# Chunked attention and token routing on one core: all comparisons on VectorE, one selection a batch, a new order of steps

## The chip, the cores and the metric

The kernel runs on one core of a Trainium2 chip. A core has TensorE (PE, matrix products), VectorE (DVE), ScalarE (ACT), GpSimd (POOL) and SyncE (SP); each works through its own queue of instructions in order, and waits on semaphores for the others. Transfers run on 16 DMA engines. The metric is the device time of one execution in microseconds; lower is better.

## The reference

Inputs are q, k, v of shape 4 x 8 x 768 x 64 (batch, head, position, width), 8 memory keys and values for each head, and for the second part a gate vector of 512, w1 (512 x 1024), w2 (1024 x 512) and the capacity 128.

```python
for c in range(24):                              # chunks of 32 queries
    l, r = max(0, 32*c - 16), min(768, 32*c + 40)
    K = concat(mem_k, k[:, :, l:r]); V = concat(mem_v, v[:, :, l:r])
    s = q[:, :, 32*c:32*c+32] @ K.T / 8
    a = exp(s - max(s)); a = a / (sum(a) + 1e-9)
    out[:, :, 32*c:32*c+32] = a @ V
x = out.transpose(0, 2, 1, 3).reshape(4, 768, 512)
for b in range(4):
    score = x[b] @ w_gate                        # 768 scores
    top = indices of the 128 largest scores
    h = relu(x[b, top] @ w1)
    x[b, top] += sigmoid(score[top])[:, None] * (h @ w2)
```

The output is x, 4 x 768 x 512 in float32.

## The kernel before

**Units of work.** The 32 heads are taken two at a time, as 16 pairs n = 0 to 15; four pairs make a batch b. Everything that is done is a step with a short name, and a long string, ORDER, lists all 600 steps as `name.number.engine` (a ACT, v DVE, g POOL, p PE, s SP). The program runs through the list once and issues the instructions of each step, so the list sets the order on every engine's queue. No scheduler moves anything afterwards.

**Loads.** LK, LQ, LV (lines 130 to 150) load keys, queries and values with GpSimd DMAs that turn float32 into float16; pairs 0 and 1 come singly, later ones two at a time (LK.2 brings pairs 2 and 3, and is called K2 below). There are five buffers of each. MK and MV add the memory rows, on SP's queue from pair 2 on. LW.0 to LW.3 (line 170) load the weights w1 and w2.

**Attention for a pair.** TQ, TK, TV (`tr`, line 285) turn q, k, v on TensorE into PSUM; QB or EQ, EK and EV evict them (`copy`, lines 119 to 125). S multiplies queries by keys, R takes the largest score of each row on VectorE, A subtracts it on TensorE, E is the exponential on ScalarE. PT turns the result, EP0 and EP1 evict it. W0 and W1 turn the value windows, with the products with the gate vector, and E0, E1, VG evict those. PV is the product with the values (SG its gate columns alone, for the last batch), RC the reciprocal of the sums, GP the part of the routing score that this pair gives, NM the normalized output. ST.b writes the batch's 768 rows to DRAM, with six DMAs on SP's queue.

**Routing for a batch b.** mSC sums the 768 scores into `scr`, 128 x 6. mB0, mB1 spread them along rows on TensorE, and mR0, mR1 evict those into `brow`, so that each partition holds all 768 scores in float32. mC0 to mC5 (`cmp_`, line 545) compare the 768 scores with six columns of `scr`, one instruction each, and write 128 x 768 values of 0 or 1; mT0 to mT5 (line 555) count them with TensorE, so that each token knows how many tokens beat it. mMK makes the mask of those with fewer than 128 above them. mIN, mLT and mSL (line 576) number the chosen ones. mSE (line 583) makes the selection matrix by comparing a row of the numbers 1 to 128 with each token's slot, in six instructions of 128 x 128. mAU reads the indices and the gate out of it, mIX and mGS evict them. mGX and mGD compute the gate 1/(1+exp(-score)): the exponential on ScalarE, then an addition, a reciprocal (on VectorE always) and two small operations (lines 534 to 537).

**The block for a batch.** For b = 0 to 2 mGI gathers the 128 chosen rows back from DRAM (GpSimd, indirect) and mGT turns them; for the last batch mG0 to mG3 gather them by products with the selection matrix from a float16 copy (XC). mX evicts, mFa and mFb (line 643) are the products with w1, mHa and mHb the relu, mYa and mYb (lines 673, 678) the products with w2, mY scales by the gate, and mSCAT (line 690) adds the rows to the output in DRAM, as an indirect DMA from GpSimd. The scatters follow one another, since they write the same tensor.

**What stood where.** Of the 24 comparisons 12 were on VectorE and 12 on GpSimd: all six of batch 0, three of batch 1, one of batch 2 and two of batch 3. The selections of batches 0 and 1 were on GpSimd, those of 2 and 3 on VectorE.

Of the kernel before, what the change touches and what calls it, by code (L numbers as in the profile page):

```python
# [8 lines left out]
FP = mybir.dt.float32  # L9
F16 = mybir.dt.float16  # L10
# [33 lines left out]
NM.8.v mR1.1.a mB0.1.p E.10.a TV.11.p EK.11.v PV.9.p mR0.1.a EK.12.v mFa.0.p EV.11.a mC2.1.v mC1.1.g
mFb.0.p RC.9.v GP.9.v mC3.1.v mHa.0.a mC0.1.g PT.10.p NM.9.v TV.12.p EP0.10.a mYa.0.p mHb.0.v S.11.p
EP1.10.v mT0.1.p mT1.1.p R.11.v mT2.1.p W0.11.p mC5.1.g mYb.0.p mC4.1.v EV.12.a PV.10.p mY.0.v mT3.1.p
mT4.1.p mT5.1.p W0.12.p RC.10.v mSCAT.0.g W1.11.p mMK.1.v E0.11.a GP.10.v TK.13.p E0.12.v E1.11.a W1.12.p
VG.11.v EK.13.v TQ.13.p E1.12.a A.11.p mIN.1.v EQ.13.v TQ.12.p TV.13.p E.11.a VG.12.v EQ.12.v mLT.1.p
TV.14.p NM.10.v EV.13.a S.12.p PT.11.p mSL.1.v R.12.v mSE.1.g S.13.p EP0.11.a TQ.14.p EV.14.v A.12.p
EP1.11.a W0.13.p E.12.a EQ.14.v TK.14.p mAU.1.p E0.13.v PT.12.p R.13.v TK.15.p PV.11.p EP0.12.a mIX.1.v  # L50
mGS.1.v mGI.1.g A.13.p RC.11.v EK.14.a GP.11.v mSC.2.v NM.11.v E.13.a mB0.2.p ST.2.s mB1.2.p mR0.2.a
mR1.2.v EP1.12.a S.14.p mC0.2.v mC2.2.g mC3.2.v mGX.2.a W1.13.p EK.15.a mC1.2.v SG.12.p mGD.2.g R.14.v
VG.13.a TQ.15.p mGT.1.p EQ.15.a E1.13.v A.14.p W0.14.p mX0.1.v W1.14.p mFb.1.p RC.12.v E0.14.v E.14.a
VG.14.v TV.15.p GP.12.v E1.14.v mT0.2.p mT1.2.p mHb.1.a mT2.2.p mT3.2.p mFa.1.p mC4.2.v EV.15.a mC5.2.v
mT4.2.p PT.13.p mT5.2.p mHa.1.a S.15.p mMK.2.v PV.12.p EP0.13.a mIN.2.v R.15.v mLT.2.p W0.15.p EP1.13.a
PT.14.p mSL.2.v A.15.p mSE.2.v EP0.14.a mYa.1.p E0.15.v E.15.a mAU.2.p EP1.14.v W1.15.p mIX.2.v PT.15.p
mGI.2.g mGS.2.v VG.15.a NM.12.v SG.13.p EP0.15.a mYb.1.p RC.13.v EP1.15.a E1.15.v SG.14.p GP.13.v mY.1.a
XC.12.g SG.15.p RC.14.v GP.14.v mSCAT.1.g RC.15.v PV.14.p GP.15.v mSC.3.v mGX.3.a mB0.3.p NM.14.v mB1.3.p
mR0.3.a mGD.3.g PV.13.p mR1.3.v mGT.2.p mC0.3.v mC1.3.g PV.15.p mC3.3.v mX0.2.a mT0.3.p NM.13.v mFa.2.p
mC2.3.g mC4.3.v mT1.3.p mFb.2.p mHa.2.a mC5.3.v XC.14.g XC.13.a NM.15.v mT2.3.p mT3.3.p mT4.3.p mT5.3.p  # L60
mYa.2.p mHb.2.a mMK.3.v mIN.3.v ST.3.s XC.15.a mLT.3.p mYb.2.p mSL.3.v mSE.3.v mY.2.a mG0.3.p mG1.3.p
mSCAT.2.g mX0.3.a mG2.3.p mX1.3.a mG3.3.p mX2.3.v mAU.3.p mX3.3.v mGS.3.v mFa.3.p mFb.3.p mHa.3.a mIX.3.v
# [8 lines left out]
def _sap(t, offset, dims):  # L71
    return bass.AP(tensor=t.tensor, offset=t.offset + offset, ap=[list(t.ap[0])] + [list(d) for d in dims])
# [3 lines left out]
def kernel(  # L76
# [280 lines left out]
    QBS = set(range(8))  # L357
# [215 lines left out]
    def mSL(b, e):  # L573
        m = mods[b]
        m.slot = mod2.tile([128, NB], FP, tag="slot", name="slot")
        nc.vector.scalar_tensor_tensor(out=m.slot, in0=m.incl, scalar=m.pn[:, 0:1], in1=m.mask,  # L576
                                       op0=ALU.add, op1=ALU.mult)

    def mSE(b, e):
        m = mods[b]  # L580
        m.sel = mod2.tile([128, NB, cap], F16, tag="sel", name="sel")
        for bl in range(NB):
            (nc.vector if e == DVE else nc.gpsimd).tensor_scalar(out=m.sel[:, bl, :], in0=iota1, scalar1=m.slot[:, bl:bl + 1],  # L583
                                                                 scalar2=None, op0=ALU.is_equal)
# [163 lines left out]
```

## Time and profile before

| | |
|---|---|
| runs shown | 154.9, 156.58, 155.77 us; median 155.77 |
| the profiled execution | 154.68 us, of which the span is 153.0 us |
| granted TensorE clock, mean | 0.877 |
| busy in the span: PE, DVE, ACT, POOL | 115.6, 98.1, 87.9, 76.5 us |
| instructions on DVE, ACT, POOL | 221, 114, 97 |
| software DMA queue: packets, MB | 12320, 13.66 |

A page of a profile shows one execution. Busy times of an engine are shares of the span in which it worked; instructions may overlap by a little at their ends, so the mean duration of one times their number is somewhat more than the busy time. Lines of groups read: source line, engine, operation, output and input tile, shapes, count, then busy time and mean nanoseconds of one, then the idle time of the engine before them and what ended it. Rows of a timeline begin with the start and the duration in microseconds, and end with the idle time before, where there was some, and its releaser. In the slices each digit is a fortieth of the span, in tenths; PEclk is the clock that TensorE was granted.

### The profile page before, as it was taken

The numbers are of one execution on the slowest core, as the hardware profiler recorded it, in microseconds if no ns is written. First come the engines' busy times: TensorE is split into PE (matmuls) and PEld (weight loads), VectorE is DVE, ScalarE is ACT, GpSimd is POOL, SyncE is SP. The second block draws the span as 40 slices with busy tenths as digits, with TensorE's granted clock in tenths as the row PEclk, the third lists the DMA queues.
The fourth block names the chain that finished last, engine by engine and source line by source line (L and its number), as shares of the span: only waits on it lengthen the run. The fifth ranks groups of instructions, "written<-read, shape, count | busy, mean of one in ns | idle before, by whom it ended". The sixth has DMA issues, their size and how long they took to land.

```text
span 153.0 us, 6101 instructions
## 1 busy us (share of the span) xinstructions
PE 115.6 (76%) x2730; PEld 95.2 (62%) x2730; DVE 98.1 (64%) x221; ACT 87.9 (57%) x114; POOL 76.5 (50%) x97
## 2 busy tenths in 40 slices
PE   0367574988689559799699998998849999489800
PEld 0256463977568458688588894976639967377500
DVE  2676562679877978061758899697874684875000
ACT  3962634386945439457499786296944774163400
POOL 6999611333211999940641178628450044983040
PEclk9999959599978955557999999999995999879995
DMA  2998999999999999999834900230570002518631
GB/s 13 163 122 155 195 230 212 205 209 208 209 207 227 287 284 216 217 188 205 139 67 143 350 9 0 20 57 4 202 280 8 4 6 66 69 43 329 112 41 27
DMA packets 16854, 21.91 MB, mean 143 GB/s; under 512 B 1774, under 2 KB 12014, under 8 KB 16829
## 3 DMA queue, kind: packets, MB, share of 16 engines
q0 software_dynamic: 12320, 13.66, 55.6%
q1 hardware_dynamic: 4509, 7.87, 15.3%
q8 instruction: 21, 0.34, 0.9%
q14 instruction: 4, 0.03, 0.1%
HBM read 26.02 MB, written 7.41 MB: 218 GB/s over the span
## 4 chain that ended last, share of the span: by engine, by line
PE 30%; POOL 26%; DMA 14%; issue 8%; ACT 8%; DVE 7%; POOLq 1%; ACTq 0%
POOL cmp L545 14%; DMA ql<-in_q_dram 8%; DMA out_dram<-y,idx 6%; PE p_w L319 3%; PE p_q L285 3%; PE p_v L319 3%; PE p_k L285 3%; PE p_v L285 3%; DVE m L398 2%; PE p_s L403 2%; PE p_x L449 2%; POOL sel L583 2%; PE p_c L555 2%; ACT vT L121 2%; PE p_y L678 2%
## 5 line engine op out<-in xcount | busy, mean ns | idle before, releaser
L545 POOL TENSOR_SCALAR cmp<-brow,scr 128x768 f16<-128x768 f32 x12 | 28.2, 2358 | 11.9 <-ACT brow L121 9.3
L121 ACT COPY pt<-p_p 64x768 f16<-64x768 f16 x19 | 15.1, 793 | 9.0 <-PE p_p L418 7.8
L410 ACT ACTIVATE P<-p_s 128x768 f16<-128x768 f32 x16 | 13.0, 811 | 10.0 <-PE p_s L403 9.8
L285 PE MATMUL p_k<-seg,kl 126*64 126x126 f16 x256 | 12.4, 256 | 6.7 <-DMA kl<-in_mem_k_dram 6.7
L121 ACT COPY vT<-p_v 128x1536 f16<-128x1536 f16 x11 | 15.6, 1440 | 2.8 <-PE p_v L285 2.8
L398 DVE TENSOR_REDUCE m<-p_s 128x12 bf16<-128x768 f32 x16 | 15.2, 951 | 1.8 <-PE p_s L386 0.8
L319 PEld LDWEIGHTS <-vT 128*128 128x128 f16 x192 | 13.6, 107 | 3.2 <-issue 1.2
L478 DVE TENSOR_TENSOR x<-p_x,rd 128x768 f32<-128x768 f32 x16 | 15.1, 946 | 0.2
L285 PEld LDWEIGHTS <-kl 126*64 126x64 f16 x256 | 10.1, 134 | 8.0 <-DMA kl<-in_k_dram 5.7
L449 PE MATMUL p_x<-vw,pt 128*64 128x66 f16 (+2 forms) x480 | 12.2, 199 | 3.7 <-DVE pt L123 2.7
L449 PEld LDWEIGHTS <-pt 128*64 128x64 f16 x480 | 10.5, 119 | 6.1 <-ACT vw L121 2.3
L285 PE MATMUL p_v<-seg,vl 126*64 126x126 f16 x256 | 12.9, 259 | 0.0
L121 ACT COPY kT<-p_k 128x1008 f16<-128x1008 f16 x10 | 10.0, 999 | 5.0 <-PE p_k L285 4.7
L123 DVE COPY qb<-p_q 64x768 f16<-64x768 f16 x14 | 7.7, 552 | 7.1 <-PE p_q L285 4.5
L583 POOL TENSOR_SCALAR sel<-iota,slot 128x128 f16<-128x128 f16 x12 | 7.0, 598 | 10.4 <-DVE slot L576 10.4
L285 PE MATMUL p_q<-ident,ql 96*64 96x96 f16 x256 | 10.0, 231 | 2.8 <-DMA ql<-in_q_dram 2.8
L403 PE MATMUL p_s<-m,negi 128*128 128x384 bf16 x32 | 9.0, 368 | 3.6 <-DVE m L398 3.6
L121 ACT COPY vw<-p_v 128x768 f16<-128x768 f16 x9 | 7.2, 803 | 7.9 <-PE p_v L329 7.0
L545 DVE TENSOR_SCALAR cmp<-brow,scr 128x768 f16<-128x768 f32 x12 | 10.3, 886 | 2.2 <-PE p_c L555 2.0
L418 PE MATMUL p_p<-perm,P 128*128 128x128 f16 x96 | 9.1, 236 | 3.3 <-DVE qb L123 3.2
L690 POOL DMA_INDIRECT out_dram<-y,idx x4 | 6.5, 1628 | 9.4 <-ACT y L684 6.9
L285 PEld LDWEIGHTS <-vl 126*64 126x64 f16 x256 | 10.2, 136 | 1.0 <-issue 0.8
(120 smaller groups left out, 251.1 us busy)
## 6 DMA issues: line engine op xcount, KB each, us to landing
out_dram<-x SPq DMA_DIRECT2D x24, 256.0 KB, 3.4
kl<-in_k_dram POOLq DMA_DIRECT2D x7, 384.0 KB, 16.1
ql<-in_q_dram POOLq DMA_DIRECT2D x7, 384.0 KB, 16.0
vl<-in_v_dram POOLq DMA_DIRECT2D x7, 384.0 KB, 17.3
w_sb<-in_moe_w_dram POOLq DMA_DIRECT2D x4, 512.0 KB, 17.7
kl<-mk SPq DMA_DIRECT2D x7, 120.0 KB, 8.4
vl<-mv SPq DMA_DIRECT2D x7, 100.0 KB
kl<-in_k_dram POOLq DMA_DIRECT2D x2, 192.0 KB, 3.8
```

The costliest lines, as they stand in the source:

```text
L121: nc.scalar.copy(out=out, in_=in_)
L123: nc.vector.tensor_copy(out=out, in_=in_)
L285: nc.tensor.transpose(out=p[64 * h:64 * h + 64, o:o + w], in_=src[n // 2 % GB][0:rows, n % 2, h, 64 * j:64 * j + 64], identity=perm)
L319: nc.tensor.transpose(out=p.bitcast(F16)[:, 128 * o:128 * o + 128], in_=pair(n, 6 * i + o), identity=ident16)
L398: nc.vector.tensor_reduce(out=s.m, in_=keys(s.s), axis=AX.X, op=ALU.max)
L403: nc.tensor.matmul(out=s.s[:, h, 0:384], lhsT=negi, rhs=s.m[:, h, :].unsqueeze(2).to_broadcast([128, NB, 64]), start=False, stop=True, ski ...
L410: nc.scalar.activation(out=s.P, in_=keys(s.s), func=AF.Exp, scale=0.125)
L418: nc.tensor.transpose(out=p[:, 128 * i:128 * i + 128], in_=s.P[:, h, 2 * bp:2 * bp + 2, :].rearrange("p b k -> p (b k)"), identity=perm16)
L449: nc.tensor.matmul(out=X[64 * cc:64 * cc + 64, c2, w * (2 * bp + h):w * (2 * bp + h) + w], lhsT=s.PT[:, i, c, :, :].rearrange("p b t -> p ...
L478: nc.vector.tensor_tensor(out=x5.rearrange("p b g (h d) -> p b g h d", d=D), in0=s.x[:, :, :, :, 0:64], in1=s.rd.unsqueeze(4).to_broadcast ...
L545: (nc.vector if e == DVE else nc.gpsimd).tensor_scalar(out=t, in0=m.brow, scalar1=m.scr[:, bl:bl + 1], scalar2=None, op0=ALU.is_lt)
L583: (nc.vector if e == DVE else nc.gpsimd).tensor_scalar(out=m.sel[:, bl, :], in0=iota1, scalar1=m.slot[:, bl:bl + 1], scalar2=None, op0=ALU ...
```

## The change

Three things change. All 24 comparisons mC0 to mC5 go to VectorE (by the letter in the list). The selection mSE is one instruction for all six columns, with the slots in float16 and broadcast along the row. And the list is a new one, from a search that works with latest times, with the same 600 steps: steps stand in another order on all engines, and some evictions have moved between VectorE and ScalarE. From VectorE to ScalarE go, net, four EP, four EQ, six QB and six VG; from ScalarE to VectorE go four EV, three EK and one of E0, E1; a few set-up steps (CP, CV, CW) move as well, both XC copies of ScalarE go to GpSimd, and batch 0's gate arithmetic mGD goes from VectorE to GpSimd. A function VX and a set VXS come in that are not used, since the set is empty.

```diff
     def mSL(b, e):
         m = mods[b]
-        m.slot = mod2.tile([128, NB], FP, tag="slot", name="slot")
+        m.slot = mod2.tile([128, NB], F16, tag="slot", name="slot")
...
     def mSE(b, e):
         m = mods[b]
         m.sel = mod2.tile([128, NB, cap], F16, tag="sel", name="sel")
-        for bl in range(NB):
-            (nc.vector if e == DVE else nc.gpsimd).tensor_scalar(out=m.sel[:, bl, :], in0=iota1, scalar1=m.slot[:, bl:bl + 1],
-                                                                 scalar2=None, op0=ALU.is_equal)
+        nc.vector.tensor_tensor(out=m.sel, in0=m.slot.unsqueeze(2).to_broadcast([128, NB, cap]),
+                                in1=iota1.unsqueeze(1).to_broadcast([128, NB, cap]), op=ALU.is_equal)
```

Of the list, three places. The loads, only the steps of GpSimd's loads shown (the old list first):

```diff
- LK.0 LQ.0 LV.0 LK.1 LQ.1 LV.1 LK.2 LQ.2 LV.2 LK.4 LQ.4 LV.4 LK.6 LQ.6 LV.6 LW.0 LK.8 LW.1 LQ.8 LW.2 LV.8 LW.3 LK.10 ...
+ LK.0 LQ.0 LV.0 LK.1 LQ.1 LV.1 LW.0 LK.2 LW.1 LQ.2 LW.2 LV.2 LW.3 LK.4 LQ.4 LV.4 LK.6 LQ.6 LV.6 LK.8 LQ.8 LV.8 LK.10 ...
```

The routing of batch 0, its own steps with their engines:

```diff
- mSC.0.v mB1.0.p mB0.0.p mR1.0.v mGX.0.a mR0.0.a mC1.0.g mGD.0.v mC2.0.g mC5.0.g mC0.0.g mT0.0.p mT1.0.p mC3.0.g mT2.0.p mC4.0.g mT3.0.p mT4.0.p mT5.0.p mMK.0.v mIN.0.v mLT.0.p mSL.0.v mSE.0.g mAU.0.p
+ mSC.0.v mB0.0.p mB1.0.p mR0.0.v mR1.0.a mC1.0.v mC0.0.v mGX.0.a mGD.0.g mC3.0.v mC4.0.v mT0.0.p mT1.0.p mC2.0.v mC5.0.v mT2.0.p mT3.0.p mT4.0.p mT5.0.p mMK.0.v mIN.0.v mLT.0.p mSL.0.v mSE.0.v mAU.0.p
```

The end, whole, from mSC.3 on:

```diff
- mSC.3.v mGX.3.a mB0.3.p NM.14.v mB1.3.p mR0.3.a mGD.3.g PV.13.p mR1.3.v mGT.2.p mC0.3.v mC1.3.g PV.15.p mC3.3.v mX0.2.a mT0.3.p NM.13.v mFa.2.p mC2.3.g mC4.3.v mT1.3.p mFb.2.p mHa.2.a mC5.3.v XC.14.g XC.13.a NM.15.v mT2.3.p mT3.3.p mT4.3.p mT5.3.p mYa.2.p mHb.2.a mMK.3.v mIN.3.v ST.3.s XC.15.a mLT.3.p mYb.2.p mSL.3.v mSE.3.v mY.2.a mG0.3.p mG1.3.p mSCAT.2.g mX0.3.a mG2.3.p mX1.3.a mG3.3.p mX2.3.v mAU.3.p mX3.3.v mGS.3.v mFa.3.p mFb.3.p mHa.3.a mIX.3.v mYa.3.p mHb.3.a mYb.3.p mY.3.a mSCAT.3.g
+ mSC.3.v NM.14.v mGX.3.a mB0.3.p mGD.3.g mB1.3.p mR0.3.a PV.15.p mR1.3.v mC0.3.v mY.1.a XC.14.g mC1.3.v mGT.2.p mSCAT.1.g mC2.3.v mT0.3.p mT1.3.p mX0.2.a mC3.3.v mT2.3.p mFa.2.p mC4.3.v mC5.3.v mT3.3.p mT4.3.p NM.15.v mT5.3.p mHa.2.a mFb.2.p mMK.3.v XC.15.g ST.3.s mIN.3.v mLT.3.p mYa.2.p mHb.2.a mSL.3.v mSE.3.v mYb.2.p mG0.3.p mY.2.a mG1.3.p mG2.3.p mX1.3.v mG3.3.p mSCAT.2.g mX0.3.v mX2.3.a mAU.3.p mX3.3.a mFa.3.p mIX.3.v mGS.3.v mFb.3.p mHa.3.v mYa.3.p mHb.3.a mYb.3.p mY.3.a mSCAT.3.g
```

In the old list mSCAT.1.g stands ahead of mSC.3 and of batch 3's gate.

More of the change, by code (lines that the diff above doesn't have):

```diff
@@ L45 @@
[L45 to L59, printed above, removed]
@@ L60 @@
[L60 to L62 removed]
+CV.0.v LK.0.g MK.0.g LQ.0.g C0.0.g LV.0.g CP.4.v CV.4.a CP.3.g CV.2.v CQ.0.a TQ.0.p MV.0.g CP.0.a LK.1.g
+CQ.1.a TK.0.p C1.0.v PM.0.g CV.1.a MK.1.g EK.0.v CP.1.a TV.0.p LQ.1.g QB0.0.v CP.2.a C2.0.g CO.0.v QB1.0.v
@@ new lines @@
+mSC.1.v TV.11.p ST.1.s R.8.v EQ.10.a mB0.1.p EP1.9.a EV.11.v A.8.p S.10.p mR0.1.a W0.10.p R.10.v E.8.a
+mGT.0.p mB1.1.p W0.11.p E0.10.v mX0.0.a A.10.p E0.11.v mR1.1.a TK.11.p mFa.0.p mC0.1.v EK.11.a mC1.1.v
+mFb.0.p mC2.1.v mHa.0.a E.10.a mC4.1.v PT.8.p PV.9.p mHb.0.a EP0.8.v S.11.p mGX.1.a RC.9.v EP1.8.a mGD.1.g
+TK.12.p NM.9.v TK.13.p EK.12.a PT.10.p GP.9.v mYa.0.p EK.13.v R.11.v mYb.0.p EP0.10.a PV.8.p EP1.10.a
+mY.0.v TQ.12.p RC.8.v mSCAT.0.g TK.14.p NM.8.v EQ.12.a A.11.p W1.10.p EK.14.v E.11.a TV.12.p W1.11.p
@@ new lines @@
+W1.14.p mSE.2.v EP0.15.a PV.13.p E1.14.v EP1.15.a mAU.2.p mYa.1.p mIX.2.v NM.13.v VG.14.a mGI.2.g SG.15.p
+SG.14.p RC.15.v GP.15.v mGS.2.v PV.14.p XC.13.g RC.14.v GP.14.v mYb.1.p mSC.3.v NM.14.v mGX.3.a mB0.3.p
+mGD.3.g mB1.3.p mR0.3.a PV.15.p mR1.3.v mC0.3.v mY.1.a XC.14.g mC1.3.v mGT.2.p mSCAT.1.g mC2.3.v mT0.3.p
+mT1.3.p mX0.2.a mC3.3.v mT2.3.p mFa.2.p mC4.3.v mC5.3.v mT3.3.p mT4.3.p NM.15.v mT5.3.p mHa.2.a mFb.2.p
+mMK.3.v XC.15.g ST.3.s mIN.3.v mLT.3.p mYa.2.p mHb.2.a mSL.3.v mSE.3.v mYb.2.p mG0.3.p mY.2.a mG1.3.p
@@ L63 @@
+mG2.3.p mX1.3.v mG3.3.p mSCAT.2.g mX0.3.v mX2.3.a mAU.3.p mX3.3.a mFa.3.p mIX.3.v mGS.3.v mFb.3.p mHa.3.v
 mYa.3.p mHb.3.a mYb.3.p mY.3.a mSCAT.3.g
@@ L355, in QB @@
                  _sap(s.pq[g], 0, [[4, NC], [96, 8], [1, 4]]))
-    QBS = set(range(8))
+    QBS, VXS = set(range(8)), set(())
     def S_(n, e):
```

67 lines of the change are left out of this document (40 added, 27 removed).

## The prediction, on record before the run

> **What bounds the kernel now.** I read the page's slices first, then the busy times by stage, then the chain of waits and the timelines of the two stages that stood out.
>
> ```profile
> span 153.0 us, 6101 instructions
> PE   0367574988689559799699998998849999489800
> PEclk9999959599978955557999999999995999879995
> DMA  2998999999999999999834900230570002518631
> ```
>
> The DMA engines are full for the first nineteen of forty slices (to about 73 us): that is the time of the loads. TensorE is busy nearly all the time after that, but with holes, and its clock is at half around slices 15 to 18. No engine is full, so I cut the span where batch 0's scores are summed (mSC.0, 44.05), where its rows are selected (mSE.0, 74.04) and where the last batch's scores are summed (mSC.3, 127.37).
>
> ```profile
> core 0: us, PE busy (x) PEld busy (x) DVE busy (x) ACT busy (x) POOL busy (x), PEclk, DMA share, GB/s
> 25.80:44.05 18.25, 14.97 (x386) 12.59 (x388) 14.91 (x29) 10.39 (x13) 6.36 (x9) 0.90 1.21 207
> 44.05:74.04 29.99, 25.33 (x542) 21.84 (x541) 18.63 (x36) 17.47 (x22) 17.81 (x13) 0.66 1.20 229
> 74.04:127.37 53.33, 48.17 (x1364) 39.58 (x1364) 41.57 (x99) 38.94 (x51) 23.88 (x27) 0.97 0.32 92
> 127.37:153.00 25.63, 14.53 (x219) 10.77 (x211) 9.22 (x23) 7.11 (x13) 11.42 (x9) 0.87 0.41 93
> 55.00:72.00 17.00, 15.92 (x308) 13.78 (x308) 8.22 (x17) 11.76 (x14) 11.80 (x9) 0.53 1.21 218
> 108.00:115.00 7.00, 4.84 (x140) 4.18 (x141) 5.81 (x11) 4.71 (x8) 3.56 (x4) 1.00 0.72 265
> 115.00:120.00 5.00, 5.00 (x98) 4.64 (x95) 2.11 (x6) 2.61 (x4) 0.00 (x0) 0.66 0.02 5
> ```
>
> The second stage is the poor one: 30 us in which VectorE and ScalarE work 18 us each and TensorE looks full only because its clock is 0.66. The chain of waits and the timeline say why.
>
> ```profile
> 51.88 2.22 POOL cmp L545
> 54.75 4.40 POOL cmp L545 x2
> 59.80 4.40 POOL cmp L545 x2
> 64.25 0.32 PE p_c L555 x6
> ```
>
> ```profile
> 51.61 2.53 DVE L536 CAST aux<-gt 128x6 f16<-128x6 f32 x1
> 55.15 0.80 PE L418 MATMUL p_p<-perm,P 128*128 128x128 f16 x6 [3.21 <-DVE qb L123]
> ```
>
> Six comparisons on GpSimd, one behind the other, carry the chain to 64.2. One of them also holds a VectorE copy of six values per partition for 2.53 us; the query eviction behind it is late, TensorE stands 3.21 us, and after that it runs at 0.53 from 55 to 72. The same happens in small near 112: a comparison holds back batch 2's gate on GpSimd, VectorE waits for the gate, and TensorE idles and then has a slow 115 to 120.
>
> ```profile
> 109.50 2.94 POOL L545 TENSOR_SCALAR cmp<-brow,scr 128x768 f16<-128x768 f32 x1 [2.08 <-DVE brow L123]
> 112.42 0.23 POOL L534 TENSOR_SCALAR gt<-gt 128x6 f32<-128x6 f32 x1
> 112.69 0.19 DVE L535 RECIPROCAL gt<-gt 128x6 f32<-128x6 f32 x1 [0.93 <-POOL gt L534]
> ```
>
> **The change part by part.** The prices, by element count and engine:
>
> ```profile
> L545 DVE TENSOR_SCALAR cmp<-brow,scr x12: 604/784/1261, 89.1 to 134.3; 128x768 f16<-128x768 f32 x12
> ```
>
> ```profile
> L545 POOL TENSOR_SCALAR cmp<-brow,scr 128x768 f16<-128x768 f32 x12 | 28.2, 2358 | 11.9 <-ACT brow L121 9.3 <-DVE brow L123 2.1 <-PE p_c L555 0.5
> L478 DVE TENSOR_TENSOR x<-p_x,rd 128x768 f32<-128x768 f32 x16 | 15.1, 946 | 0.2
> L123 DVE COPY pt<-p_p 64x768 f16<-64x768 f16 x13 | 7.2, 555 | 4.5 <-ACT pt L121 2.5 <-PE p_p L418 1.7
> L583 POOL TENSOR_SCALAR sel<-iota,slot 128x128 f16<-128x128 f16 x12 | 7.0, 598 | 10.4 <-DVE slot L576 10.4
> L123 DVE COPY vT<-p_v 128x1536 f16<-128x1536 f16 x5 | 5.3, 1051 | 0.9 <-PE p_v L285 0.8
> L123 DVE COPY kT<-p_k 128x1008 f16<-128x1008 f16 x6 | 4.0, 674 | 0.4 <-PE p_k L285 0.4
> L468 DVE RECIPROCAL rd<-p_x 128x12 f32<-128x12 f32 x16 | 3.6, 227 | 4.0 <-PE p_x L449 3.9
> L123 DVE CAST vw<-p_v 128x24 f16<-128x24 f32 x11 | 2.9, 260 | 1.9 <-ACT vw L121 1.6 <-PE p_v L329 0.3
> L472 DVE TENSOR_TENSOR scp<-p_x,rd 128x12 f32<-128x12 f32 x16 | 2.7, 167 | 0.3
> ```
>
> Comparisons: GpSimd loses 12 (28.2 us) and VectorE gains 12. Its own took 0.604 to 1.261 us, the median 0.784. I take 0.784, since the slow ones ran beside GpSimd's, which are gone: +9.4 us on VectorE, bounds +7.2 and +15.1. Selection: six instructions a batch become one over 768 values. No row shows that form; it lies between the fastest comparison (0.604) and the 768-wide product (0.946), and I take 0.946, the only row with two tensor inputs. GpSimd loses its 7.0 us. These are loads on engines; the path is decided by the order, which I price by stage.
>
> *Stage A, start to mSC.0.* The new order issues all four weight loads ahead of LK.4; the old one began them after LV.6. GpSimd's issues are paced by landings, eight transfers deep, which shows what each load costs:
>
> ```profile
> 26.05 0.73 POOL L172 DMA_DIRECT2D w_sb<-in_moe_w_dram  x1 [4.44 <-DMA ql<-in_q_dram]
> 29.60 0.71 POOL L172 DMA_DIRECT2D w_sb<-in_moe_w_dram  x1 [1.20 <-DMA kl<-in_k_dram]
> 37.75 0.75 POOL L176 DMA_DIRECT2D w_sb<-in_moe_w_dram  x1 [1.67 <-DMA ql<-in_q_dram]
> 42.37 0.67 POOL L138 DMA_DIRECT2D ql<-in_q_dram  x1 [1.72 <-DMA w_sb<-in_moe_w_dram]
> ```
>
> K4 landed by 29.60, and the four loads behind it (Q4, V4, K6, Q6) by 37.75: about 2.0 us each. V6 and the first weight load landed between 37.75 and 42.37, 4.6 us, so a weight load costs about 2.6 to 2.7 us (not less than 2.0). Four of them put K4 at 29.6 + 4 x 2.7 = 40.4. The queue is full in both orders, so nothing hides this while TensorE needs K4. From TK.4 to mSC.0 the new list has on VectorE 5 of the 768-wide operations (R, NM) at 0.946, 8 copies at 0.555, one EV at 1.051, two EK at 0.674 and two pairs RC, GP at 0.39: 12.4 us; with about 0.7 for waits mSC.0 falls at 53.5, 9.5 later than now. Less of the work is then behind it by that clock, but the new list also puts more ahead of mSC.0 (51 TensorE steps against 44).
>
> *Stage B, mSC.0 to mSE.0.* On VectorE now six comparisons (4.7), five R and NM (4.7), seven copies (3.9), two EV (2.1), one EK (0.7), three RC, GP (1.2), two VG (0.5), and six small ones (1.2): 19.0 us, nothing of it waiting for GpSimd. With 1.3 for waits 20.3 instead of 29.99: -9.7. The gate is on GpSimd with no comparison beside it, so the 2.53 us are gone; what is late next is VectorE itself. A and B together: -0.2, mSE.0 at 73.8. The TensorE steps left after it are nearly the same in both lists.
>
> *Stage C, mSE.0 to mSC.3.* Gone: the idle part of 108 to 115 (7.00 - 4.84 = 2.2) and the slow clock after it (5.00 x 0.34 = 1.7), -3.9. VectorE's work there changes by four more comparisons (+3.1), two EV (+2.1), one R (+0.95), eight copies fewer (-4.4) and five VG fewer (-1.3), +0.4; the other moves (two whole selections for six small ones, a relu and an eviction to ScalarE) cancel to under 1 us. C: -3.5.
>
> *Stage D, the tail.*
>
> ```profile
> 127.37 0.20 DVE L498 TENSOR_REDUCE scr<-scp 128x6 f32<-128x48 f32 x1
> 130.67 0.38 DVE L123 COPY brow<-p_b 128x256 f32<-128x256 f32 x1
> 134.09 1.87 PE L643 MATMUL p_h<-xeT,w_sb 128*128 128x128 f16 x16
> 137.26 0.17 DVE L561 TENSOR_SCALAR mask<-p_c 128x6 f32<-128x6 f32 x1 [0.87 <-PE p_c L555]
> ```
>
> Now the mask comes 9.9 us after the last score sum. In the new order VectorE has in between 0.2, NM 0.95, the row copy 0.38, six comparisons 4.7 and NM 0.95: 7.2, 2.7 earlier. But mFb.2 (1.87) moves behind the counts, in front of mLT.3. Net -0.8. The gate (mGD.3) is moved ahead of the scatter mSCAT.1 on GpSimd, so it no longer waits behind that issue. The last scatter still starts when its result is ready, and the end behind it stays.
>
> Sum: -0.2 - 3.5 - 0.8 = -4.5 on a span of 153.0. The profiled execution took 154.68, 1.68 around its span; that gives 150.2. The median of the three runs is 155.77, 1.09 above the profiled one: 151.3.
>
> **The rivals.**
>
> *Slower: the early weights leave TensorE at low clock.* TensorE must wait for Q2, V2 and K4 in turn. If the wait for K4 drops the clock as the 3.21 us wait before 55 did, and it stays at 0.53 for 17 us as it did there, the 24 TensorE steps from TK.4 to mSC.0 take twice as long: the 27 steps of 25.80 to 44.05 took 14.97 us at 0.90, so 24 take 13.3, and 13.3 x 0.90 / 0.53 = 22.6 at low clock. mSC.0 falls at 63, the whole at 151.3 + 9.5 = 160.8. It decides from about 10 us at low clock on (each loses 0.47, and 4.5 is to be lost). For it: 55 to 72, where TensorE was busy 15.92 of 17.00 and stayed slow. Against it: 115 to 120, where the slow time ended within 5 us.
> The Trainium skill, TensorE: Matmul & The Clock Gate, Part 1, says that a window of about 3.4 us of sustained activity returns the clock to full. By that rule a low clock after K4 costs an estimated 1.7 us and this rival falls away, so the sum would be 153.0; by the row of 55 to 72 it is 160.8. The trace agrees with the rule after 115 and differs from it after 55, and the measurement decides.
>
> *Faster still: the weights are hidden.* If TensorE does not wait for K4, stage A grows only by its seven more steps, 7 x 0.555 = 3.9 instead of 9.5: 151.3 - 5.6 = 145.7. For it: TK.4 has slack of some microseconds now. Against: at 40.4 the slack is used up.
>
> *No change: the waits come back elsewhere.* VectorE takes 9 us more, and it is the first engine in stages A and B; if B needs 24 us (VectorE 80% busy, near the 78% of 74.04 to 127.37) and one new hole of TensorE takes the place of the one near 112 (3.9), the gain is gone: 151.3 + 3.7 + 3.9 = 158.9, or about 155 when only one of the two happens.
>
> **How the numbers follow.** The forecast, 151.3, has 0.43; the low clock 0.18; hidden weights 0.15; no change 0.24, two thirds of it with one mishap (155) and one third with both (159). About 1% is what a measurement of this kernel can tell from no change: below 154.2 is faster, above 157.3 slower. Faster: 0.43 less 0.03 that drifts up, plus 0.15, 0.55. Within 1%: 0.03 plus 0.16, 0.19. Slower: 0.18 plus 0.08, 0.26. The range leaves out the lowest part of the hidden weights and most of the low clock: 146.5 to 158.5, which also takes in the bounds of the comparison's price (-2 and +6 us on VectorE). The forecast's own range is 148.5 to 154.
>
> **What would show it.** A: the first TensorE step on K4 starts near 40, mSC.0 near 53; at 48 the weights were hidden, at 60 the low clock won. B: comparisons on VectorE at 0.6 to 0.8 us, no VectorE instruction on six values over 1 us, 20 us from mSC.0 to mSE.0. C: no hole of TensorE over 2 us between mSE.0 and mSC.3, and that stage under 50 us. D: the mask 7 us after the last score sum. The single selection takes 0.6 to 0.95 us. I am wrong if weights turn out cheaper than 2 us each, or if stage B is not shorter than 25 us.

## The result, and the profile after

The changed kernel takes 149.33 us in the median of four executions (148.14 to 150.93), the kernel before 156.18 in four (154.9 to 156.9): a ratio of 0.9545, with a 95% interval from 0.9433 to 0.9657. The ratio is taken over the fast executions alone, those within 1.5% of the quickest of their kernel. It is faster, by 6.85 us in the medians. The profiled execution of the changed kernel was the slowest of its four (150.93, span 149.2) and that of before (154.68) below all of its own, so the two spans differ by only 3.8 us.

The page of the changed kernel, its first line and three of its rows of slices:

```profile
span 149.2 us, 6081 instructions
PE   0078406777697958847998999999989988889700
PEclk9999955675799999998579999999999996899985
DMA  2999999999999999999942580060192002069631
```

The longest slow clock has changed its place: before it stood around slices 15 to 18 (counted from 0), now, with one gap, in slices 5 to 10 (19 to 41 us) and, shorter, in 19 and 20 (71 to 78 us). The DMA engines are full for the first nineteen slices, as before. The loads have kept their volume; only their order is another.

Busy times by stage, cut at the same steps as before (mSC.0, mSE.0, mSC.3), and four stretches that are needed below:

```profile
core 0: us, PE busy (x) PEld busy (x) DVE busy (x) ACT busy (x) POOL busy (x), PEclk, DMA share, GB/s
0.00:52.21 52.21, 31.29 (x729) 26.77 (x730) 32.85 (x68) 28.94 (x37) 24.45 (x49) 0.84 1.10 180
52.21:76.03 23.82, 18.16 (x429) 15.44 (x427) 16.59 (x36) 16.89 (x25) 4.41 (x7) 0.86 1.11 228
76.03:124.54 48.51, 45.72 (x1386) 37.78 (x1384) 41.18 (x87) 39.61 (x58) 8.17 (x12) 0.99 0.32 92
124.54:149.20 24.66, 14.93 (x203) 10.55 (x199) 9.29 (x20) 5.68 (x11) 7.48 (x8) 0.85 0.46 106
20.00:40.00 20.00, 12.49 (x260) 10.63 (x262) 10.10 (x17) 7.13 (x8) 5.47 (x9) 0.61 1.23 204
40.00:50.00 10.00, 9.18 (x282) 8.24 (x276) 8.32 (x16) 7.79 (x12) 3.50 (x6) 1.00 1.24 206
70.00:75.00 5.00, 5.00 (x119) 4.71 (x113) 3.16 (x11) 3.31 (x6) 0.00 (x0) 0.50 1.03 172
75.00:80.00 5.00, 4.61 (x140) 3.77 (x140) 4.35 (x6) 4.38 (x7) 0.00 (x0) 0.86 0.41 69
```

| stage | before | after | difference | predicted |
|---|---|---|---|---|
| A, start to mSC.0 | 44.05 | 52.21 | +8.16 | +9.5 |
| B, mSC.0 to mSE.0 | 29.99 | 23.82 | -6.17 | -9.7 |
| C, mSE.0 to mSC.3 | 53.33 | 48.51 | -4.82 | -3.5 |
| D, mSC.3 to the end | 25.63 | 24.66 | -0.97 | -0.8 |
| sum | 153.0 | 149.2 | -3.8 | -4.5 |

The first stage loses what the second and a part of the third gain. GpSimd's share of stage B falls from 17.81 to 4.41 us, and VectorE's too, from 18.63 to 16.59, although it now has six comparisons there that it did not have. The cast that took 2.53 us there is gone from VectorE, some other work has left the stage, and the comparisons are cheap, as their group on the page says:

```profile
L556 DVE TENSOR_SCALAR cmp<-brow,scr 128x768 f16<-128x768 f32 x24 | 13.4, 614 | 3.2 <-PE p_c L566 3.0
```

All 24 comparisons together take VectorE 13.4 us, 0.614 each on average; before, the twelve had a median of 0.784, up to 1.261. In VectorE's timeline the marks of the stages, one comparison of batch 0, and the tail:

```profile
52.21 0.19 DVE L509 TENSOR_REDUCE scr<-scp 128x6 f32<-128x48 f32 x1
69.70 1.15 DVE L556 TENSOR_SCALAR cmp<-brow,scr 128x768 f16<-128x768 f32 x2 [2.57 <-PE p_c L566]
76.03 0.95 DVE L593 TENSOR_TENSOR sel<-slot,iota 128x768 f16<-128x768 f16 x1
124.54 0.20 DVE L509 TENSOR_REDUCE scr<-scp 128x6 f32<-128x48 f32 x1
127.95 0.42 DVE L123 COPY brow<-p_b 128x256 f32<-128x256 f32 x1 [1.85 <-PE p_b L515]
132.53 0.15 DVE L572 TENSOR_SCALAR mask<-p_c 128x6 f32<-128x6 f32 x1
```

The selection takes 0.95 us, and the last mask comes 8.0 us after the last score sum (9.9 before). The second line is the new wait of stage B: the last two comparisons of batch 0 wait 2.57 us for the counts on TensorE that read the comparisons before them. TensorE's timeline shows what held it:

```profile
39.67 1.07 PE L285 MATMUL p_k<-seg,kl 126*64 126x126 f16 x32 [1.19 <-DMA kl<-in_k_dram]
53.78 0.43 PE L285 MATMUL p_v<-seg,vl 126*64 126x126 f16 x9 [1.50 <-issue]
60.17 0.41 PE L285 MATMUL p_k<-seg,kl 126*64 126x126 f16 x8 [0.41 <-issue]
64.56 0.36 PE L285 MATMUL p_v<-seg,vl 126*64 126x126 f16 x6
67.17 0.47 PE L285 MATMUL p_v<-seg,vl 126*64 126x126 f16 x10 [2.26 <-issue]
69.03 0.51 PE L429 MATMUL p_p<-perm,P 128*128 128x128 f16 x6 [0.95 <-ACT P L421]
```

The transposition of one pair's values is a step of sixteen equal products. It stops after six of them for 2.26 us, with its data at hand, and "issue" says that the profile shows nothing it waited for. The same happens at 52.3 (1.50) and, in a step on keys, at 59.8 (0.41). In the profile of before TensorE has no wait of this kind. It is the place where the forecast of stage B went wrong, and the experiments go after it.

### The profile page after: what moved, and what is told of

It reads as the page before. It is cut to its first block, busy times and chain, and to the rows that moved or that the text cites. A ratio compares the mean times of both kernels' runs of the same rounds, so it can differ in the third digit from the quotient of the medians.

```text
span 149.2 us, 6081 instructions
## 1 busy us (share of the span) xinstructions
PE 110.1 (74%) x2730; PEld 90.5 (61%) x2730; DVE 99.9 (67%) x207; ACT 91.1 (61%) x129; POOL 44.5 (30%) x76
## 4 chain that ended last, share of the span: by engine, by line
PE 40%; DMA 24%; DVE 18%; issue 8%; POOL 3%; ACT 2%; POOLq 1%; DVEq 0%; ACTq 0%
DMA kl<-in_k_dram 11%; DMA w_sb<-in_moe_w_dram 10%; PE p_x L460 5%; DVE cmp L556 5%; PE p_k L285 3%; PE p_v L285 3%; PE p_w L330 3%; DMA out_dram<-y,idx 3%; PE p_s L414 3%; PE p_v L330 3%; PE p_s L397 3%; DVE m L409 2%; PE p_q L285 2%; PE p_y L688 2%; DVE x L489 2%
## 5 line engine op out<-in xcount | busy, mean ns | idle before, releaser
L121 ACT COPY pt<-p_p 64x768 f16<-64x768 f16 x23 | 18.3, 796 | 2.6 <-PE p_p L429 2.0
L285 PE MATMUL p_v<-seg,vl 126*64 126x126 f16 x256 | 12.0, 243 | 10.7 <-DMA vl<-in_mem_v_dram 6.0
L285 PEld LDWEIGHTS <-vl 126*64 126x64 f16 x256 | 9.1, 124 | 12.4 <-issue 10.7
L123 DVE COPY vT<-p_v 128x1536 f16<-128x1536 f16 x9 | 9.5, 1054 | 9.1 <-PE p_v L285 9.0
L556 DVE TENSOR_SCALAR cmp<-brow,scr 128x768 f16<-128x768 f32 x24 | 13.4, 614 | 3.2 <-PE p_c L566 3.0
L285 PEld LDWEIGHTS <-ql 96*64 96x64 f16 x256 | 7.4, 120 | 10.3 <-DMA ql<-in_q_dram 9.2
L622 POOL DMA_INDIRECT xg<-out_dram,idx x3 | 3.2, 1056 | 32.6 <-DVE idx L606 32.6
L121 ACT COPY vT<-p_v 128x1536 f16<-128x1536 f16 x7 | 10.1, 1439 | 3.0 <-PE p_v L285 3.0
L330 PE MATMUL p_w<-ident,vT 128*128 128x128 f16 x96 | 9.3, 242 | 0.1
L330 PE MATMUL p_v<-ident,vT 128*128 128x128 f16 x96 | 9.1, 237 | 0.0
```

The costliest lines, as they stand in the source:

```text
L121: nc.scalar.copy(out=out, in_=in_)
L123: nc.vector.tensor_copy(out=out, in_=in_)
L285: nc.tensor.transpose(out=p[64 * h:64 * h + 64, o:o + w], in_=src[n // 2 % GB][0:rows, n % 2, h, 64 * j:64 * j + 64], identity=perm)
L330: nc.tensor.transpose(out=p.bitcast(F16)[:, 128 * o:128 * o + 128], in_=pair(n, 6 * i + o), identity=ident16)
L556: (nc.vector if e == DVE else nc.gpsimd).tensor_scalar(out=t, in0=m.brow, scalar1=m.scr[:, bl:bl + 1], scalar2=None, op0=ALU.is_lt)
```

## The experiments

The theory after the result: moving the comparisons away from GpSimd brings the gain; the early weights cost 8 us of it; the order matters only with the comparisons. Against it stand that the new order brings it, that the single selection does, or that the weights cost nothing since other waits would fill the time. The kernel before ran in each of the three sets too: 155.76, 156.92 and 156.6 us. For the first set the medians are given with their lowest and highest, without an interval.

### The changed kernel again

No edit.

> The changed kernel once more, beside the others on the same chip. All theories: about 149.3 us against 156.2 before, ratio 0.945 to 0.965. In a profile with fewer low-clock stretches, stage B (from the score sum of batch 0 to its selection) should be 19 to 22 us instead of the 23.8 of the first profile, and the other stages the same.

148.6 us (146.6 to 149.86). The stages are 53.75, 23.61, 47.17 and 22.87 us on a span of 147.4. Stage B at 19 to 22 was missed again: two executions agree, so 23.6 to 23.8 is what this order takes. The third stop is there again (2.26 us), and the half clock behind it (0.50 from 72 to 77). The slow clock of 20 to 40 us is not: here it was 1.00 in that stretch, and mSC.0 came no earlier for it. The mask came 6.5 us after the last score sum.

### The comparisons alone

The old list with the engine letter of twelve comparisons changed; six selections, weights and everything else as before.

```diff
- mC1.0.g mGD.0.v mC2.0.g mC5.0.g mC0.0.g ... mC3.0.g ... mC4.0.g
+ mC1.0.v mGD.0.v mC2.0.v mC5.0.v mC0.0.v ... mC3.0.v ... mC4.0.v
```

> The old order with nothing changed but the twelve comparisons that were on GpSimd, which go to VectorE at their old places. Theory 1 (comparisons on GpSimd carried the chain of stage B and held VectorE up near 112): stage B falls from 30 us to 23 to 25, the 2.53 us copy of six values is gone, total 150 to 152.5. Theory 2 (the gain is the new order's, and twelve more comparisons at 0.61 us are 7.4 us more for VectorE): 155.5 to 158.

150.86 us (148.93 to 152.74) against 155.76 (153.0 to 156.82): 4.9 less, and the two ranges do not overlap. In the old order stage B falls from 29.99 to 25.85 us (45.59 to 71.44), not quite to the 23 to 25 that were expected, and batch 0's cast takes 0.18 us. So most of the whole gain needs no new order. TensorE now has stops on "issue" in the old order too, where the kernel before had none:

```profile
63.80 0.36 PE L281 MATMUL p_q<-ident,ql 96*64 96x96 f16 x8 [0.82 <-issue]
69.73 0.43 PE L382 MATMUL p_s<-kT,qT 64*32 64x64 f16 x33 [0.97 <-issue]
```

### The new order with the comparisons back on GpSimd

```diff
- mC1.0.v mC0.0.v ... mC3.0.v mC4.0.v ... mC2.0.v mC5.0.v
+ mC1.0.g mC0.0.g ... mC3.0.g mC4.0.g ... mC2.0.g mC5.0.g
```

and so for the other six that GpSimd had before.

> The new order with the same twelve comparisons back on GpSimd. Theory 1: stage B back to 27 to 31 us, a comparison again holding a VectorE instruction for over 1 us, total 154 to 157. Theory 2: within 1 us of the changed kernel, 148.5 to 150.5, since the order hides them.

159.5 us (157.37 to 159.92): 10.9 slower than the changed kernel in the same set and 3.7 slower than the kernel before. The sign was expected, the size not. The comparisons by engine, from the view of the tile `cmp` (shortest, median and longest in ns, then the first and last start), two rows of VectorE's timeline and the busy times of stage B and of the tail:

```profile
L552 POOL TENSOR_SCALAR cmp<-brow,scr x12: 2191/2212/2962, 56.0 to 132.4; 128x768 f16<-128x768 f32 x12
L552 DVE TENSOR_SCALAR cmp<-brow,scr x12: 609/621/1384, 88.4 to 131.5; 128x768 f16<-128x768 f32 x12
```

```profile
61.42 0.19 DVE L542 RECIPROCAL gt<-gt 128x6 f32<-128x6 f32 x1 [4.15 <-POOL gt L541]
74.60 0.17 DVE L568 TENSOR_SCALAR mask<-p_c 128x6 f32<-128x6 f32 x1 [2.96 <-PE p_c L562]
```

```profile
52.14:77.03 24.89, 17.02 (x429) 14.12 (x427) 13.60 (x31) 16.80 (x25) 17.16 (x14) 0.97 1.09 220
125.65:155.60 29.95, 15.03 (x197) 11.37 (x191) 9.20 (x18) 5.66 (x11) 12.23 (x11) 0.80 0.39 88
```

The waits are back (4.15 us for the gate behind a comparison, 2.96 for the mask), but stage B does not go back to the 27 to 31 us that were expected: it takes 24.89, only 1.1 more than in the changed kernel. The loss is in the tail, 29.95 us instead of 24.66: the mask of batch 3 there comes 12.2 us after the last score sum instead of 8.0, having waited 4.08 us for the counts. With the comparisons on GpSimd the new order is worse than the old one. In stage B either part of the change, the comparisons in the old order (25.85) or the new order with them on GpSimd (24.89), brings most of the gain, and both together hardly more (23.82).

### The comparisons and the single selection in the old order

```diff
- mSE.0.g
+ mSE.0.v
```

and so for the other batches, with the new instruction over 768 values and its float16 slots.

> The old order with all comparisons on VectorE and the single selection on VectorE for every batch: parts one and two of the change without the third. With the comparisons alone it was 150.9. On GpSimd the six selections took 3.5 us, and what waits for them (mAU, the gather) is behind other work of TensorE. Theory S (selections on GpSimd were hidden): 150 to 151.5, and the new order is worth the last 1.5 to 2.5 us. Rival (they were on the path): 148 to 149.5, and the new order is worth nothing by itself.

150.51 us (150.07 to 151.84), a ratio of 0.97 [0.9557, 0.9843]. Beside 150.86 without it (in another set, whose kernel before was 1.2 us quicker), the selection in the old order brings nothing that shows.

### Six selections in the new order

```diff
-        nc.vector.tensor_tensor(out=m.sel, in0=m.slot.unsqueeze(2).to_broadcast([128, NB, cap]), ...)
+        for bl in range(NB):
+            nc.vector.tensor_scalar(out=m.sel[:, bl, :], in0=iota1, scalar1=m.slot[:, bl:bl + 1],
+                                    scalar2=None, op0=ALU.is_equal)
```

> The changed kernel with the selection in six instructions of 128 x 128 on VectorE and float32 slots, as the old kernel had it for batches 2 and 3. The old form took 1.06 us for the six, the single one takes 0.95 us, so all theories expect no measurable difference: 148 to 150, within 0.5 us of the changed kernel.

149.04 us (148.26 to 150.63), 0.9553 [0.9434, 0.9673]; the change has 0.9545. Six small selections on VectorE take 1.06 us together, the single one 0.95. As expected, no difference.

### Early weights in the old order

```diff
- LV.1 LK.2 LQ.2 LV.2 LK.4 LQ.4 LV.4 LK.6 LQ.6 LV.6 LW.0 LK.8 LW.1 LQ.8 LW.2 LV.8 LW.3
+ LV.1 LW.0 LK.2 LW.1 LQ.2 LW.2 LV.2 LW.3 LK.4 LQ.4 LV.4 LK.6 LQ.6 LV.6 LK.8 LQ.8 LV.8
```

> The old order with nothing changed but the four weight loads, which go ahead of LK.4 as in the new one. Theory A (early weights put back the first pairs by 8 to 10 us): the first TensorE step on K4 starts at 41 to 43 instead of 35.4, the score sum of batch 0 at 50 to 53 instead of 44, and since the comparisons on GpSimd follow it, the total rises by 3 to 8 us: 159 to 164. Rival (the old order's stage B has room that takes it up): 155 to 157.

166.75 us (166.06 to 167.93), 1.074 [1.0589, 1.0892]: 9.8 slower than before, more than expected. Batch 0's score sum, and the wait for the query eviction that the prediction showed in the kernel before:

```profile
55.25 0.20 DVE L494 TENSOR_REDUCE scr<-scp 128x6 f32<-128x48 f32 x1
```

```profile
64.87 0.49 PE L414 MATMUL p_p<-perm,P 128*128 128x128 f16 x6 [3.20 <-DVE qb L119]
```

mSC.0 moves from 44.05 to 55.25, and everything behind it, the 3.2 us wait too, moves along. The cost of early weights in the old order is thus shown by itself, with no other part of the change.

### The weights last, in the new order

```diff
- LV.1 LW.0 LK.2 LW.1 LQ.2 LW.2 LV.2 LW.3 LK.4 ... LV.14
+ LV.1 LK.2 LQ.2 LV.2 LK.4 ... LV.14 LW.0 LW.1 LW.2 LW.3
```

> The new order with the four weight loads moved behind the last load of values. Theory A (the weights ahead of K4 cost stage A some 8 us that nothing gives back): the first TensorE step on K4 starts near 30 instead of 39.7, the score sum of batch 0 near 46 instead of 52.2, total 143 to 146. Rival (stage A would then be held by VectorE and ScalarE, or the later pairs' loads hold stage B): score sum at 49 or later, total 148 to 150.

147.0 us (146.39 to 147.71). The stages at the start are as expected: K4's first step on TensorE at 31.19, mSC.0 at 46.19, mSE.0 at 66.76, that is 6.0 and 9.3 earlier than in the changed kernel's profile. The total of 143 to 146 was missed: against the changed kernel in the same set, 148.6 (146.6 to 149.86), only 1.6 is left, and the ranges overlap. The lead is given back between mSC.1 and mSE.1, which takes 29.3 us (75.27 to 104.57), against 23.9 in the changed kernel. GpSimd's timeline and TensorE's show the first gather and its first use:

```profile
71.19 1.10 POOL L618 DMA_INDIRECT xg<-out_dram,idx  x1 [7.67 <-DVE idx L602]
```

```profile
82.36 1.09 PE L625 MATMUL p_e<-ident,xg 128*128 128x128 f32 x4 [2.94 <-DMA xg<-out_dram,idx]
```

The gather is issued 11 us ahead of its use and is still not there: GpSimd has issued loads and weights before it, and the reading is that it lands behind them. TensorE's wait of 2.94 us for it is a part of the 5.4 us; another is a stop of 0.90 us on "issue".

### The weights at their old places, in the new order

```diff
- LV.1 LW.0 LK.2 LW.1 LQ.2 LW.2 LV.2 LW.3 LK.4 ... LV.6 LK.8 LQ.8 LV.8
+ LV.1 LK.2 LQ.2 LV.2 LK.4 ... LV.6 LW.0 LK.8 LW.1 LQ.8 LW.2 LV.8 LW.3
```

> The new order with the weight loads where the old one had them, from behind LV.6 on. Theory A: first TensorE step on K4 near 30, score sum of batch 0 near 46 to 48, gather of batch 0 not held by loads for more than 4 us, total 144.5 to 147, as good as or better than the weights last (147.0). Rival (the loads of pairs 8 and 9 behind the weights now hold stage B): score sum at 46 to 48 but the selection of batch 0 later than 70, total 147 to 149.

147.89 us, but from 142.67 to 150.45. Inconclusive in the total. In the profile mSC.0 stands at 47.70, and the gather is late once more:

```profile
84.31 1.09 PE L625 MATMUL p_e<-ident,xg 128*128 128x128 f32 x4 [3.29 <-DMA xg<-out_dram,idx]
```

### The weights in the middle, and the last loads behind the first gather

```diff
- LV.1 LW.0 LK.2 LW.1 LQ.2 LW.2 LV.2 LW.3 LK.4 ... LV.10 ... LK.14 LQ.14 LV.14 ... mGI.0
+ LV.1 LK.2 LQ.2 LV.2 LK.4 ... LV.10 LW.0 LW.1 LW.2 LW.3 ... mGI.0 LK.14 LQ.14 LV.14
```

> The new order with the weight loads behind LV.10 and the loads of pairs 14 and 15 behind batch 0's gather mGI.0. With the weights last, the gather was issued at 71.2 and TensorE stood for it until 82.4. Theory G (the gather waits in the DMA queues behind loads that were issued before it): here it lands within 5 us of its issue, the hole near 82 is gone, total 143 to 145.5. Rival (the weights last gained little because VectorE and ScalarE bound the middle): 146.5 to 148, as with the weights last.

147.23 us (144.61 to 149.03), 0.9305 [0.914, 0.9469]. The gather, issued at 74.21, is used at 79.31 with no wait for it, as the theory of the queue has it (the weights were moved, too). The total is above what it gave, and TensorE has new stops on "issue", now where the moved loads run:

```profile
82.40 1.96 PE L649 MATMUL p_h<-xeT,w_sb 128*128 128x128 f16 x32 [1.04 <-issue]
88.71 0.86 PE L281 MATMUL p_k<-seg,kl 126*64 126x126 f16 x15 [2.42 <-issue]
```

A mixed answer: the gather is cured, but mSC.1 to mSE.1 still takes 28.7 us, since the stops of 1.04 and 2.42 us stand where the wait for the gather was.

### The weights behind V8, and the last loads behind the first gather

```diff
- LV.1 LW.0 LK.2 LW.1 LQ.2 LW.2 LV.2 LW.3 LK.4 ... LV.8 ... LK.14 LQ.14 LV.14 ... mGI.0
+ LV.1 LK.2 LQ.2 LV.2 LK.4 ... LV.8 LW.0 LW.1 LW.2 LW.3 ... mGI.0 LK.14 LQ.14 LV.14
```

> The new order with the weight loads behind LV.8 and the loads of pairs 14 and 15 behind batch 0's gather: near the version with the weights behind LV.10 (147.2, 144.6 to 149.0). Theory G (once the gather is free of the loads, the middle is held by VectorE, ScalarE and the stops of TensorE under full DMA engines): 145 to 147.5, no better. Rival (the place of the weights still matters by several us): below 144.

145.06 us (143.0 to 147.98), 0.9236 [0.9114, 0.9359]: within what was expected, and the quickest version of the whole computation here. Its interval lies below that of the change (0.9433 to 0.9657). VectorE's marks and TensorE's last three stops:

```profile
45.29 0.19 DVE L505 TENSOR_REDUCE scr<-scp 128x6 f32<-128x48 f32 x1
67.69 0.95 DVE L589 TENSOR_TENSOR sel<-slot,iota 128x768 f16<-128x768 f16 x1
```

```profile
59.15 0.49 PE L281 MATMUL p_v<-seg,vl 126*64 126x126 f16 x11 [1.99 <-issue]
83.09 1.96 PE L649 MATMUL p_h<-xeT,w_sb 128*128 128x128 f16 x32 [1.29 <-issue]
89.11 0.60 PE L281 MATMUL p_k<-seg,kl 126*64 126x126 f16 x15 [2.13 <-issue]
```

mSC.0 comes 6.9 us earlier than in the changed kernel's profile and mSE.0 8.3 earlier; by the medians about half of that reaches the end. TensorE has seven stops on "issue" of 0.39 to 2.13 us, 9.1 us in all; those after 59 us are shown.

### The memory values of pair 1 ahead of the weights

In the changed kernel TensorE waits 6.04 us near 20 for the memory rows of pair 1's values.

```diff
- LV.1 LW.0 ... MV.1
+ LV.1 MV.1 LW.0 ...
```

> The changed kernel with the memory rows of pair 1's values (MV.1) issued ahead of the first weight load instead of behind it. TensorE stands 6 to 7 us for them (TV.1 at 23.7). Theory A (the chain of stage A is K4's landing at 39.7, and this hole lies ahead of it): TV.1 starts by 20, K4 still at 39 to 40, total within 1 us of the changed kernel, 147.6 to 150. Rival (the hole is on the path): 3 to 5 us less, 144 to 146.

147.61 us (146.85 to 149.0), 0.9482 [0.9398, 0.9566], not to be told from the change. TensorE's timeline says where the wait went:

```profile
30.27 0.85 PE L281 MATMUL p_q<-ident,ql 96*64 96x96 f16 x16 [8.50 <-DMA ql<-in_q_dram]
```

It now waits 8.50 us for Q2, and K4 comes at 38.91, as good as unchanged. While the weights are in front, the holes only change their names.

### No late loads

The loads and memory rows of pairs 12 to 15 are left out, so these pairs work on data of older ones. All other instructions stay.

```diff
- LK.12 LQ.12 LV.12 MK.12 MV.12 LK.14 LQ.14 LV.14 MK.14 MV.14
```

> The changed kernel without the loads of pairs 12 to 15 (LK, LQ, LV and MK, MV with 12 and 14 left out; these pairs work on older data in their buffers). In the changed kernel TensorE stops four times between 47 and 65 us in the middle of a group of like instructions with nothing to wait for, 0.29 to 2.26 us, about 255 instructions apart, while the DMA engines are full. Theory I (its instructions come in blocks of 16 KB by the same DMA engines and are late while these are full): without the late loads the engines are free from about 58 us, the stop of 2.26 us at 65 is under 0.3 us, the low clock from 70 to 75 is gone, stage B falls from 23.6 to 19 to 21 us, total 143 to 146. Rival (the stops have another cause): the stop at 65 stays, total 147.5 to 149.5.

142.49 us (141.18 to 144.34), 0.9115 [0.9029, 0.9201]. The page's row of the DMA engines, the busy times of stage B, and every stop of TensorE in it on "issue":

```profile
DMA  2999999999999999941000490050077002079531
```

```profile
53.59:73.37 19.78, 16.39 (x442) 13.83 (x439) 16.59 (x37) 16.86 (x25) 1.67 (x3) 1.00 0.47 129
```

```profile
55.16 0.43 PE L281 MATMUL p_v<-seg,vl 126*64 126x126 f16 x9 [1.50 <-issue]
61.55 0.41 PE L281 MATMUL p_k<-seg,kl 126*64 126x126 f16 x8 [0.40 <-issue]
```

With the same work on VectorE (16.59 us) and ScalarE, stage B takes 19.78 us instead of 23.82. The first two stops, at the same steps, are as long as before (1.50, 0.40); the DMA engines are full at the first and still partly busy at the second (the slices after 57 us). The third, 2.26 us in the changed kernel, came at 65; here the engines are nearly idle by then and it is gone, and with it the slow clock: 1.00 over the stage against 0.86. That the third stop depends on the transfers is thereby shown. (Smaller stops come later, one of 0.76 us at 96.7.)

## Why the prediction was right, and where not

**The total.** 151.3 was forecast, 4.5 below the median of before; 149.33 came, 6.85 below. By stage the repeat of the changed kernel has +9.7, -6.4, -6.2 and -2.8, so A and the sign of every stage hold in both profiles; B gained less than forecast, C and D more. That the sum came near is in part luck, since these errors have opposite signs.

**What bounded the kernel: right for the old order.** The chain through GpSimd's comparisons was the thing to remove. With them alone moved, 4.9 of the 156 us go; with them alone put back, 10.9 return, though mostly in the tail and not in stage B.

**Stage A: right.** K4's first step was forecast near 40.4 and came at 39.67, mSC.0 at 53.5 and came at 52.21. The price of four weight loads was read from the pacing of GpSimd's issues; in the old order it was then measured as 11.2 us at mSC.0 and 9.8 at the end. With the weights last, K4's first step came 8.5 us earlier than in the changed kernel.

**Stage B: the step that failed.** The step put it as 19.0 us of VectorE work plus 1.3 us of waits, "what is late next is VectorE itself", 20.3 us. VectorE was busy for 16.59 us, 2.4 less than forecast. Of this 1.7 is only counting: the forecast added mean durations, and the rows, which overlap at their ends, add up to 18.3. By that sum the rest of the stage was 5.5 us instead of 1.3. The next late engine was not VectorE but TensorE, with three stops on "issue" (1.50, 0.41, 2.26 us) and the half clock from 70 to 75 behind the last. The run without late loads, where the third stop and that half clock are gone, takes 19.8 us, near the forecast's 20.3. The gate, which the step called free of GpSimd's comparisons, was: batch 0's cast of six values, 2.53 us on VectorE before, takes 0.20 on GpSimd.

**The comparison's price: too high.** 0.784 us was taken since those of VectorE that took longest ran beside GpSimd's; but as GpSimd's went away, the bound of 0.604 was the nearer one. And the step priced only the twelve that were added: VectorE's own twelve became quicker as well (0.886 on average before). 24 at 0.614 are 14.7 us; less the old twelve's 10.6 this is +4.1 us on VectorE instead of +9.4, below the lower bound of +7.2. This and stage B's stops are errors of opposite sign.

**Stage C: right, a little small.** No hole of TensorE over 2 us, as forecast (the longest on the timeline is 0.48), the clock 0.99, and 48.51 us, under the 50. It gained 1.3 us more than forecast (2.6 in the repeat), which would fit the comparisons' lower price; no run separates that.

**Stage D: the sign right, the size open.** -0.97 instead of -0.8, but -2.8 in the repeat. The mask took 8.0 us instead of 7.2, since the row copy waits 1.85 us for the spreading on TensorE, a term that was left out; in the repeat that wait is 0.56 us and the mask takes 6.5. The six comparisons take 3.3 us there, not 4.7.

**The selection: right.** 0.95 us as priced, and without a measurable effect on the time.

**The rivals.** The low clock after K4 did not come about: K4 was waited for 1.19 us only, and 40 to 50 ran at 1.00, though 20 to 40 had run at 0.61. That earlier low clock cost nothing that shows: the repeat ran 20 to 40 at 1.00 and had mSC.0 at 53.75, not sooner, with a longer wait for K4. The clock did fall later, behind the 2.26 us stop, and was back to 0.86 on average in 75 to 80; the 17 us at 0.53 of the kernel before did not recur. The Trainium skill, TensorE: Matmul & The Clock Gate, Part 1, gives about 3.4 us of activity for the way up and as much idleness for the way down; the trace agrees at 40, where the 1.19 us wait left the clock at 1.00, and differs at 70, where a stop of 2.26 us and a wait of 0.95 were enough to halve it. The hidden weights did not come about either; the 145.7 us of that rival is near what moving the weights measured, 147.0 with them last and 145.06 behind V8, where the last loads moved as well. Part of that nearness is chance: with the weights last mSC.0 came at 46.2, earlier than the rival's 48, and later stages gave it back. Of "the waits come back elsewhere" the half happened that names stage B at 24 us, 23.82, though through TensorE's stops and not through VectorE's load; the second hole in stage C did not come.

**The order's own share.** The comparisons and the selection in the old order stand at 0.97 [0.9557, 0.9843], the whole change at 0.9545 [0.9433, 0.9657]: the new order adds about 1.5%, with intervals that overlap. It holds a cost and a gain: the early weights, some 4 us by the run with them behind V8 (which also moved the last loads), and other moves that would then be worth more than that; they were not separated.

**What stays open.** Executions of one kernel differ by 1 to 8 us (most by 2 to 4), so the order among the three versions with the weights between V6 and V10 is not settled. With the weights behind V8 the lead over the changed kernel's profile is 8.3 us at mSE.0, 6.8 at mSC.1, 3.1 at mSE.1 and 4.2 at mSC.3. It is lost mostly between mSC.1 and mSE.1, which takes 27.6 us instead of 23.9, and there the stops of 1.29 and 2.13 us lie; the smaller loss before it is not explained.

## What to carry to other kernels

Take work off a slow engine where it carries the chain, even onto an engine that is busier, and price it for the state after the move, when the neighbour that slowed it is gone. While the DMA queues are full, the order of transfers is the schedule: what is fetched before it is needed delays what is needed, and a small gather can wait behind loads that were issued before it. An order and the engines for which it was made belong together: either half alone can be worth less, or cost. Where an engine stops with nothing to wait for, count its instructions from stop to stop and look at the instruction queue's packets.

## What the runs showed of the hardware that was not expected

**TensorE stops for its own instructions.** The first steps after the four stops on "issue" of the changed kernel between 47 and 67 us start at 47.71 (0.29 us of waiting before it), 53.78, 60.17 and 67.17. From stop to stop there are 254, 254 and 256 weight loads and products counted together, and 256, 256 and 257 rows with the few others of TensorE's queue. The page has a queue for instructions:

```profile
q8 instruction: 21, 0.34, 0.9%
```

Its 21 packets carry 0.34 MB, 16 KB each. The Trainium skill, Runtime: NRT & Kernel Launch, Instruction fetch mechanics, says that an engine's instructions are fetched in blocks of 16 KiB, 256 instructions, over a DMA queue of their own, and that the cost of crossing a block's end is mostly hidden. The trace agrees with the block's size, and differs on the cost, as the times of these packets show; the trace keeps them, though the views printed here do not list them. Those ahead of the four stops begin at 45.28, 51.36, 57.82 and 64.49 and take 0.94, 0.98, 0.96 and 1.40 us, and each stop ends 1.3 to 1.5 us after its packet is through. In all fourteen traces together TensorE has 40 stops of 0.5 us or more on "issue", and every one ends 1.2 to 1.7 us after such a packet. While the DMA engines are full, these four packets begin 6.1 to 6.7 us apart, and what TensorE needs less for a block it stands still. Without the late loads the packet after the one at 59.13 begins at 62.72, 3.6 us later, and the third stop is gone. So the stops are waits for late instructions; why a packet comes no sooner while the engines are full is not shown.

The kernel before fits that, too: from 55 to 72 us it ran 308 products and as many weight loads, at half clock, which is 256 rows in 17.0 x 256 / 616 = 7.1 us, and had no stop. With the comparisons alone moved, the old order ran that stretch at a clock of 1.00, and had two stops there. A quicker TensorE thus meets a limit that the slow clock had hidden.

**A comparison can be slower beside its twin.** VectorE's comparison takes 0.605 to 0.621 us in the changed kernel, with none on GpSimd, and up to 1.384 us with twelve on GpSimd (1.261 in the kernel before). In these two traces with twelve on GpSimd all ten VectorE comparisons of 0.9 us or more ran while GpSimd compared. Nine others overlapped one as well and took 0.60 to 0.63 us; what decides between the two is not shown.
